# From the fourth block of tiles on, a pair of hidden cells is computed by seven half products

## The chip, the cores and the metric

The kernel runs on one core of a Trainium2 chip. Five engines work side by side and wait for each other by semaphores: PE (TensorE, matrix products into PSUM), ACT (ScalarE), DVE (VectorE), POOL (GpSimd) and SP (SyncE, which issues most transfers). The metric is the device time of one execution in microseconds (us); smaller is better.

## What is computed

A banded attention over 8 batches x 8 heads x 576 positions (head size 64, window 64), then a feed-forward layer on the 4608 tokens that it leaves:

```python
scores = np.where(mask, q @ k.transpose(0, 1, 3, 2) / 8.0, -1e9)   # mask: 0 <= i - j < 64
x = (softmax(scores) @ v).transpose(0, 2, 1, 3).reshape(4608, 512)
h = x @ w_in                                         # 512 x 2048
g = np.maximum(h, 0.0) + alpha * np.minimum(h, 0.0)
out = g @ w_out                                      # 2048 x 512
```

The weights are given in float64 and come to the chip as pairs of 32-bit words.

## The kernel before

**Tiles and blocks.** The 4608 tokens are 36 tiles of 128; four tiles are a block (`NBLK`), so there are nine blocks, numbered here from 0. The hidden size of 2048 is 16 slices f of 128 (`NF`). A *cell* is one block and one f (in block 0, for f below `PAIRS` = 4, two cells of two tiles each).

**A product in three parts.** x, w_in, w_out and g are each kept as a high part rounded to the matmul's format and a low part, the rest (`xh`/`xl`, `win_h`/`win_l`, `wout_h`/`wout_l`, `gh`/`gl`). A product is high x high + low x high + high x low. `weights` makes the parts of w_in and w_out from the 64-bit words in the first 130 us or so, and they stay in SBUF.

**A cell** (`cell`, L718) is this chain. PE: `hidden` (L726), 3 parts x 4 chunks of the contraction = 12 matmuls of a 128x128 weight with a moving operand of 512 tokens, into one PSUM bank `h`. ACT: `slopes` (L735) writes alpha times h to SBUF. DVE: `most` (L742) takes the larger of that and h. ACT: `high` (L748) rounds it to `gh`. POOL: `rest` (L752) makes `gl`. PE: `outs` (L757), 4 tiles x 3 parts = 12 matmuls of 512 columns that add to the four tiles' `o` banks over all f. After f = 15 ACT or DVE copies each `o` to SBUF and SP stores it. Four PSUM banks (4 to 7) are for `h`, scores and attention values, four for `o`.

**Attention of a tile** (`attend`, L474): PE scores (L571, many small matmuls), eight masks with row minimum on DVE (L605), eight exponentials on ACT (L611), a scale on POOL (L632), 12 transposes on DVE (L672), PE values `av` (L690), then `xh` on ACT (L694) and `xl` on DVE (L697). The tiles of block n are taken two at a time in blocks n - 2 and n - 1, at the places in `stays`.

**Order.** All steps are handed to a planner (`Plan`, L119) with an engine, a duration written in the code, predecessors and buffers. It lays them out in time, and the instructions are emitted in the order of the planned starts, so each engine's order is fixed before the run. For the steps of the first block, the weights and the first eight tiles, deadlines come from the table `DUE`. Waits on the chip are semaphores that the framework derives from which tiles an instruction reads and writes.

Of the kernel before, what the change touches and what calls it, by code (L numbers as in the profile page):

```python
# [278 lines left out]
def banded_attention_then_prelu_ffn(  # L279
# [438 lines left out]
    def cell(ts, f, want_h, want_o):  # L718
        plan.group = "c", f, ts[0]
        n = len(ts)  # L720
        nt = n * P
        d = {}
        xs = slice((ts[0] % RING) * P, (ts[0] % RING) * P + nt)
        hb, gb, ghb, glb = Buffer("bank", 1), Buffer("g", 1), Buffer("gh", 1), Buffer("gl", 1)

        def hidden(_):  # L726
            d["h"] = ph = bank(hb, [P, NBLK * P], F32, f"h_{ts[0]}_{f}")
            k = 0
            for wt, xt in (("win_h", xh), ("win_h", xl), ("win_l", xh)):
                for c in range(NP):  # L730
                    nc.tensor.matmul(ph[:, :nt], weight(wt, f)[:, c * P:(c + 1) * P], xt[:, c, xs],  # L731
                                     start=(k == 0), stop=(k == 3 * NP - 1))
                    k += 1
# [210 lines left out]
```

## Time and profile before

| | |
|---|---|
| median of 3 runs | 891.82 us (891.49 to 892.58) |
| the profiled execution, its own time | 889.84 us |
| its span, first to last instruction | 888.1 us |
| busy share of the span | PE 99%, DVE 48%, ACT 43%, POOL 36% |
| transfers | 69.8 MB, mean 79 GB/s |

The busy share of PE counts overlapping matmuls as they are modelled; what a matmul costs in a row of them is the distance from one start to the next, which the chain of work shows as a sum over its pieces. The chain is followed back from the last instruction, so a piece in it is time that the end of the kernel waits for. The rows themselves stand in the section after the change.

### The profile page before, as it was taken

To read this page: it belongs to the slowest core of one execution; us is meant where nothing else is said; L and a number is where in the kernel's file an instruction comes from. 1 tells how busy PE (TensorE), PEld (TensorE's weight loads), DVE (VectorE), ACT (ScalarE), POOL (GpSimd) and SP (SyncE) were. 2 spreads that over 40 slices of the span, in tenths; PEclk is the share of its full clock that TensorE was granted. 3 is DMA by queue.
4 is the path that set the end of the run, shared out by engine and by line. 5 is a ranking of instruction groups with operands and counts; after the bars stand their busy time and mean duration, and the time that the engine had idled before them with its cause. 6 is when DMAs were issued, how large, how long until landed. Compare 5 with 4: busy or idle time off the path is not lost.

```text
span 888.1 us, 17218 instructions
## 1 busy us (share of the span) xinstructions
PE 881.9 (99%) x6785; PEld 731.7 (82%) x6785; DVE 423.3 (48%) x1326; ACT 378.5 (43%) x1023; POOL 322.1 (36%) x293
## 2 busy tenths in 40 slices
PE   9999999999999999999999999999999999999998
PEld 8888888888888888888888888888888888888886
DVE  6989864767262634444362617172535345111111
ACT  7888855424342434242433324253424252222222
POOL 5878743333333333323241333233333222222221
PEclk9999999999999999999999999999999999999999
DMA  9656743313130304030220213031303030001001
GB/s 325 213 189 199 240 136 102 70 40 90 66 90 18 91 30 126 18 91 18 79 77 26 66 66 90 18 90 66 90 18 90 18 97 1 1 1 48 1 1 48
DMA packets 55393, 69.80 MB, mean 79 GB/s; under 512 B 3456, under 2 KB 48784, under 8 KB 55312
## 3 DMA queue, kind: packets, MB, share of 16 engines
q1 hardware_dynamic: 54576, 68.04, 25.2%
q8 instruction: 53, 0.87, 0.4%
q10 hardware_dynamic: 736, 0.66, 0.2%
q14 instruction: 28, 0.23, 0.1%
HBM read 59.25 MB, written 9.44 MB: 77 GB/s over the span
## 4 chain that ended last, share of the span: by engine, by line
PE 98%; DVE 1%; ACT 0%; issue 0%; POOL 0%; ACTq 0%; DVEq 0%; POOLq 0%
PE h L731 44%; PE o L769 44%; PE av L690 4%; PE s L571 3%; PE s L553 1%; PE spare L363 1%; PE t L649 1%; DVE w L595 0%; ACT w L601 0%; DVE two L398 0%; ACT pt L654 0%; POOL w L632 0%; DVE rc L627 0%; DVE xl L697 0%; DVE val L415 0%
## 5 line engine op out<-in xcount | busy, mean ns | idle before, releaser
L754 POOL TENSOR_TENSOR gl<-g,gh 128x512 fp32r<-128x512 f32 x128 | 165.1, 1290 | 367.9 <-ACT gh L750 228.4
L744 DVE SCALAR_TENSOR_TENSOR g<-h,s_sb,g 128x512 f32<-128x512 f32 x128 | 96.0, 751 | 305.8 <-ACT g L737 305.7
L769 PE MATMUL o<-wout_h,gh 128*128 128x512 f32 x576 | 225.3, 391 | 0.0
L769 PE MATMUL o<-wout_l,gh 128*128 128x512 f32 x576 | 224.3, 389 | 0.0
L737 ACT ACTIVATE g<-h,sa_sb 128x512 f32<-128x512 f32 (+1 forms) x148 | 100.2, 677 | 245.3 <-PE h L731 223.8
L769 PE MATMUL o<-wout_h,gl 128*128 128x512 f32 x576 | 159.1, 389 | 0.0
L731 PE MATMUL h<-xh,win_h 128*128 128x512 f32 (+1 forms) x592 | 157.3, 388 | 0.0
L731 PE MATMUL h<-xl,win_h 128*128 128x512 f32 (+1 forms) x592 | 155.0, 384 | 0.0
L731 PE MATMUL h<-xh,win_l 128*128 128x512 f32 (+1 forms) x592 | 154.8, 383 | 0.0
L750 ACT CAST gh<-g 128x512 fp32r<-128x512 f32 x128 | 79.4, 620 | 130.4 <-DVE g L744 78.4
L672 DVE STREAM_TRANSPOSE pt<-w 32x256 f32<-32x256 f32 x312 | 130.1, 428 | 4.6 <-POOL w L632 0.9
L731 PEld LDWEIGHTS h<-xl,win_h 128*128 128x128 f32 x592 | 109.5, 188 | 22.2
L731 PEld LDWEIGHTS h<-xh,win_l 128*128 128x128 f32 x592 | 109.5, 188 | 21.9
L731 PEld LDWEIGHTS h<-xh,win_h 128*128 128x128 f32 x592 | 108.2, 188 | 23.2 <-DVE gl L754 0.2
L769 PEld LDWEIGHTS o<-wout_h,gh 128*128 128x128 f32 x576 | 108.1, 188 | 22.7 <-issue 0.5
L769 PEld LDWEIGHTS o<-wout_h,gl 128*128 128x128 f32 x576 | 108.1, 188 | 22.6
L769 PEld LDWEIGHTS o<-wout_l,gh 128*128 128x128 f32 x576 | 108.2, 188 | 22.1
L611 ACT ACTIVATE w<-w,nm 128x96 f32<-128x96 f32 x208 | 75.5, 365 | 93.1 <-DVE nm L605 93.1
L632 POOL TENSOR_TENSOR w<-w,rc 128x768 f32<-128x768 f32 (+2 forms) x44 | 59.3, 1348 | 137.9 <-ACT w L611 105.9
L605 DVE CUSTOM_DVE_ANT_0 w<-s,masks 128x96 f32<-128x96 f32 x184 | 34.4, 253 | 91.1 <-PE s L571 91.1
L419 POOL TENSOR_TENSOR val<-val,low 128x512 int32<-128x512 int32 x32 | 41.2, 1293 | 13.2 <-DVE val L415 7.6
L690 PE MATMUL av<-pt,v 128*64 128x64 f32 x1152 | 38.8, 224 | 0.5 <-ACT pt L654 0.5
(65 smaller groups left out, 593.5 us busy)
## 6 DMA issues: line engine op xcount, KB each, us to landing
v<-vN SPq DMA_DIRECT2D x72, 256.0 KB, 4.5
k<-kT SPq DMA_DIRECT2D x35, 384.0 KB, 5.1
out<-os SPq DMA_DIRECT2D x35, 256.0 KB, 2.1
q<-qT SPq DMA_DIRECT2D x34, 256.0 KB, 6.2
raw<-w_in SPq DMA_DIRECT2D x16, 512.0 KB, 4.6
raw<-w_out SPq DMA_DIRECT2D x16, 512.0 KB, 3.9
k<-kT SPq DMA_DIRECT2D x2, 192.0 KB, 3.2
q<-qT ACTq DMA_DIRECT2D x2, 128.0 KB, 3.4
```

What stands on the lines that cost most here:

```text
L419: nc.gpsimd.tensor_tensor(out=d["val"], in0=d["val"], in1=d["tail"], op=ALU.add)
L605: nc.vector.tensor_tensor_reduce(out=d["w"][:, e, h], in0=d["s", e][:, h], in1=slim[begins], op0=ALU.add, op1=ALU.min, scale=-SCALE, scala ...
L611: nc.scalar.activation(w, w, AF.Exp, scale=-1.0, bias=d["nm"][:, g:g + 1], accum_out=d["sm"][:, g:g + 1])
L632: nc.gpsimd.tensor_tensor(out=w, in0=w, in1=d["rc"][:, g].unsqueeze(2).broadcast_to(list(w.shape)), op=ALU.mult)
L672: nc.vector.transpose(dst[:, :, i * SUB:(i + 1) * SUB], d["w"][r, :, :, k * SUB:(k + 1) * SUB].rearrange("p e h k -> p (e h) k"))
L690: nc.tensor.matmul(av[r, e, u * W:(u + 1) * W], d["v"][:, e, u, r], d["pt"][:, u * NP + e, h * W:(h + 1) * W], start=True, stop=True)
L731: nc.tensor.matmul(ph[:, :nt], weight(wt, f)[:, c * P:(c + 1) * P], xt[:, c, xs], start=(k == 0), stop=(k == 3 * NP - 1))
L737: nc.scalar.activation(d["g"], d["h"][:, :nt], AF.Copy, scale=sa_sb[:, f:f + 1])
L744: nc.vector.scalar_tensor_tensor(out=g, in0=d["h"][:, :nt], scalar=s_sb[:, f:f + 1], in1=d["g"], op0=ALU.mult, op1=ALU.max)
L750: nc.scalar.copy(d["gh"], d["g"])
L754: (nc.vector if start else nc.gpsimd).tensor_tensor(out=d["gl"], in0=d["g"], in1=d["gh"].bitcast(F32), op=ALU.subtract)
L769: nc.tensor.matmul(po[t], gt[:, i * P:(i + 1) * P], weight(wt, f), start=(f == 0 and k == 0), stop=(f == NF - 1 and k == 2))
```

## The change

From block 3 on (`W0`), two neighbouring cells f and f + 1 are one `pair`. h is then a 2 x 2 of blocks (two slices f, two halves of 256 tokens), and the contraction has two halves of 256; the eight half products of such a 2 x 2 are replaced by seven, in Winograd's form of Strassen's algorithm, whose operands are sums of blocks of w_in and sums of blocks of x. A half product (`product`) is 3 parts x 2 chunks = 6 matmuls of a 128x128 weight with 256 tokens.

*Sums of w_in.* `combine`, once for each of the eight pairs of slices, after block 0: the four sums are formed on POOL and DVE, split into parts on ACT and POOL or DVE, and SP writes them to a DRAM tile `kept`, five entries of 256 KB in all for a pair of slices. In each of the six blocks each pair reads its five entries back (`load`, 240 reads) into five buffers. The part of the resident w_in that is no longer read becomes room for these and for the sums of x.

*Sums of x.* In `attend`, for every second tile from tile 13 on, DVE forms sums of x (`t_one`, `t_two`), and ACT and DVE split them (`t_high`, `t_low`); the even tile's PSUM bank is kept until then.

*A pair* has two banks: bank X holds a (right half) and b (left half), bank Y holds c (right half) and d (left half). The products are emitted on PE in the order p12 (two: into a, and into b), p7 (into d), p6 (onto a), p4 (onto d), p5 (onto a), p3 (onto a). Between them ACT copies half a bank to SBUF (`spare`, 128x256), and DVE adds it (`add`, 128x256): c1 copies a after p12 and v1 adds it to b; c7 copies d after p7; c6 copies a after p6; v2 makes c from a after p5; v3 adds to d after p4. `behind` is the old chain of a cell after `hidden`; in a pair its `outs` is cut in three steps.

```diff
+W0 = 3
+SHORT = 93.0
+TSETS = (0, 3)
+LAGS = (16.0, 19.0)
...
+    dram = ctx.enter_context(tc.tile_pool(name="dram", bufs=1, space=bass.MemoryType.DRAM))
...
-        ab, xb = Buffer("bank", 1), Buffer(f"x{t % RING}", 1)
+        paired = t >= W0 * NBLK
+        slot = t // NBLK % 2 * NBLK + ((0, 2, 1, 3)[t % NBLK] if paired else t % NBLK)
+        ab, xb = Buffer("bank", 1), Buffer(f"x{slot}", 1)
         d["x"] = xb
-        xs = slice((t % RING) * P, (t % RING + 1) * P)
+        xs = slice(slot * P, (slot + 1) * P)
...
-        hi = step({ACT: (0.47, 0.59)}, x_high, [va], take=[xb])
-        return scores, va, step({DVE: (0.6, 0.69)}, x_low, [hi], give=[ab], want=want)
+        d["va"], d["ab"] = va, ab
+        if not paired:
+            hi = step({ACT: (0.47, 0.59)}, x_high, [va], take=[xb])
+            return scores, va, step({DVE: (0.6, 0.69)}, x_low, [hi], give=[ab], want=want)
+        if t % 2 == 0:
+            hi = step({ACT: (0.47, 0.59)}, x_high, [va], take=[xb])
+            d["low"] = step({DVE: (0.6, 0.69)}, x_low, [hi], want=want)
+            return scores, va, d["low"]
...
+        def whole(_):
+            d["x32"] = room(xt, [P, E], F32, f"x32_{t}")
+            nc.scalar.copy(d["x32"], d["av"].rearrange("p k w -> p (k w)"))
+        def t_one(_):
+            a, b, (x1, _x2) = d0["av"], d["av"], halves()
+            sub(a[:, 0:2], x1, a[:, 0:2])
+            sub(b[:, 0:2], b[:, 2:4], x1)
+
+        def t_two(_):
+            a, (_x1, x2) = d0["av"], halves()
+            sub(x2, x2, a[:, 0:2])
+            sub(a[:, 2:4], a[:, 2:4], x2)
+        def t_high(m):
+            nc.scalar.copy(turns("win_h", q0 + (m == 1) * 2, m), pieces(m))
+        def t_low(m):
+            q = q0 + (m == 1) * 2
+            sub(turns("win_l", q, m), pieces(m), turns("win_h", q, m).bitcast(F32))
+        w0 = step({ACT: (0.48, 0.59)}, whole, [va], take=[xt])
+        one = step({DVE: (0.78, 0.88)}, t_one, [d0["va"], w0, d0["low"]])
+        hi = step({ACT: (0.47, 0.59)}, x_high, [one], take=[xb])
+        two = step({DVE: (0.78, 0.88)}, t_two, [one])
+        lo = step({DVE: (0.6, 0.69)}, x_low, [hi], give=[ab])
+        ha = step({ACT: (0.47, 0.59)}, lambda _: t_high(2), [two], take=[tsets[n]] if j == 0 else [])
+        hb = step({ACT: (0.28, 0.39)}, lambda _: t_high(1), [two], [ha])
+        la = step({DVE: (0.6, 0.69)}, lambda _: t_low(2), [ha, lo], give=[d0["ab"]], want=want)
+        lb = step({DVE: (0.33, 0.42)}, lambda _: t_low(1), [hb, la], give=[xt], want=want)
+        return scores, va, lb
...
+    def behind(ts, f, d, done, hb, want_o, cols, coarse=True):
...
+        every = [(i, k) for i in range(n) for k in (0, 1, 2)]
+        gh_ones, gl_ones = [x for x in every if x[1] < 2], [x for x in every if x[1] == 2]
+        if f == NF - 1:
+            todos = [every] if coarse else [every[j:j + 3] for j in range(0, 3 * n, 3)]
+        else:
+            todos = [gh_ones + gl_ones] if coarse else [gh_ones[:4], gh_ones[4:], gl_ones]
...
+        for todo in todos:
+            lows = any(k == 2 for _, k in todo)
+            h = 0.68 * n if coarse else 0.2267 * len(todo)
+            own = sorted({ts[i] for i, k in todo if f == 0 and k == 0})
+            s5 = step({PE: (h, h + 0.1)}, lambda _, todo=todo: outs(todo),
+                      [s3] + [s4] * lows + cv[2 * f + 1]["done"], take=[ob[t] for t in own],
+                      give=[ghb] + [glb] * lows, want=want_o)
...
+    def combine(q):
+        plan.group = "s", q, 2 * NBLK
+        d = {}
...
+        def total(e, i):
+            d[i] = room(bufs[i], [P, E], F32, f"sum_{q}_{i}")
+            (nc.gpsimd if e == POOL else nc.vector).tensor_tensor(
+                out=d[i], in0=weight("win_h", f + i).bitcast(F32), in1=weight("win_l", f + i).bitcast(F32), op=ALU.add)
+
+        def sums(_):
+            a11, a12, a21, a22 = d[0][:, :2 * P], d[0][:, 2 * P:], d[1][:, :2 * P], d[1][:, 2 * P:]
+            nc.vector.tensor_tensor(out=a22, in0=a21, in1=a22, op=ALU.add)
+            nc.vector.tensor_tensor(out=a21, in0=a11, in1=a21, op=ALU.subtract)
+            nc.vector.tensor_tensor(out=a11, in0=a22, in1=a11, op=ALU.subtract)
...
+        entries[q] = dram.tile([P, 5, 2, 2 * P], F32, name=f"kept_{q}")
+        t0 = step({POOL: (1.22, 1.28), DVE: (0.59, 0.68)}, lambda e: total(e, 0), done, begun[-NBLK:],
+                  take=bufs + taken.get(q, []), give=regions[q], port=True)
+        begun.append(t0)
+        t1 = step({POOL: (1.22, 1.28), DVE: (0.59, 0.68)}, lambda e: total(e, 1), [*done, t0], give=regions[q], port=True)
+        su = step({DVE: (1.35, 1.45)}, sums, [t0, t1], port=True)
+        out = [step({SP: (0.4, 0.4)}, lambda _, low=low: keep(2, low), done, [t0], give=regions[q], moved=0.6, span=0.8)
+               for low in (0, 1)]
+        for i in range(2):
+            hi = step({ACT: (0.51, 0.61)}, lambda _, i=i: high(i), [su])
+            lo = step({POOL: (1.22, 1.28), DVE: (0.59, 0.68)}, lambda e, i=i: rest(e, i), [hi], port=True)
+            out.append(step({SP: (0.4, 0.4)}, lambda _, i=i: keep(i, 0), [hi], give=[bufs[2 + i]], moved=0.9))
+            out.append(step({SP: (0.4, 0.4)}, lambda _, i=i: keep(i, 1), [lo], give=[bufs[i]], moved=0.9))
+        kept[q] = out
+
...
+    def pair(ts, q, want):
+        plan.group = "c", 2 * q, ts[0]
+        n = ts[0] // NBLK
+        f = 2 * q
+        dx, dy, d = {}, {}, {}
+        bx, by, u2 = Buffer("bank", 1), Buffer("bank", 1), Buffer("u2", 1)
+        left = slice(ts[0] % RING * P, ts[0] % RING * P + 2 * P)
+        right = slice(left.stop, left.stop + 2 * P)
+        q0 = TSETS[(n - W0) % 2]
+
+        def load(e):
+            def fetch(_):
+                where = b.at
+                d[e] = (region("win_" + where[0], where[1]) if isinstance(where, tuple) else
+                        room(b, [P, E], F32R, f"stream_{n}_{q}_{e}"))
+                nc.sync.dma_start(d[e].bitcast(F32).rearrange("p (l c) -> p l c", l=2), entries[q][:, e])
+
+            s = step({SP: (0.4, 0.4)}, fetch, kept[q], loaded[-1:], take=[b], moved=0.85, span=1.1)
+            loaded.append(s)
+            return s, b
...
+        def product(out, w, x, start):
+            todo = [(w[i], x[j]) for i, j in ((0, 0), (0, 1), (1, 0))]
+            for i, (a, b) in enumerate(todo):
+                for c in range(2):
+                    nc.tensor.matmul(out, a[:, c * P:(c + 1) * P], b[c], start=start and i == c == 0,
+                                     stop=i == 2 and c == 1, skip_group_check=True)
+
+        def p12(_):
+            dx["h"] = bank(bx, [P, NBLK * P], F32, f"h_{ts[0]}_{f}")
+            d["b"], d["a"] = dx["h"][:, :2 * P], dx["h"][:, 2 * P:]
+            product(d["a"], own(0, 0), tokens(0, left), True)
+            product(d["b"], streamed(0), tokens(1, left), False)
+
+        def p7(_):
+            dy["h"] = bank(by, [P, NBLK * P], F32, f"h_{ts[0]}_{f + 1}")
+            d["d"], d["c"] = dy["h"][:, :2 * P], dy["h"][:, 2 * P:]
+            product(d["d"], streamed(3), tokens(0, right), True)
+
+        def p6(_):
+            product(d["a"], streamed(1), turned(2), False)
+
+        def p5(_):
+            product(d["a"], streamed(4), turned(0), False)
+
+        def p3(_):
+            product(d["a"], streamed(2), tokens(1, right), False)
+
+        def p4(_):
+            product(d["d"], own(1, 1), turned(1), False)
+
+        def add(out, a, b):
+            nc.vector.tensor_tensor(out=out, in0=a, in1=b, op=ALU.add)
+
+        def spare(i, x):
+            if "u" not in d:
+                d["u"] = room(u2, [P, E], F32, f"u_{n}_{q}")
+                d["u"] = d["u"][:, :2 * P], d["u"][:, 2 * P:]
+            nc.scalar.copy(d["u"][i], d[x])
...
+        one = {PE: (0.72, 0.87)}
+        s12 = step({PE: (1.44, 1.59)}, p12, [st_done[t] for t in ts] + [l0], take=[bx], give=[b0, x0, x2], want=want)
+        s7 = step(one, p7, [l3], [s12], take=[by], give=[b3, x1, x3], want=want + 1.0)
+        c1 = step({ACT: (0.28, 0.39)}, lambda _: spare(1, "a"), [s12], take=[u2])
+        c7 = step({ACT: (0.28, 0.39)}, lambda _: spare(0, "d"), [s7], [c1])
+        v1 = step({DVE: (0.38, 0.48)}, lambda _: add(d["b"], d["b"], d["u"][1]), [c1])
+        s6 = step(one, p6, [c1, l1], [s7], give=[b1, tsets[n]], want=want + 2.0)
+        c6 = step({ACT: (0.28, 0.39)}, lambda _: spare(1, "a"), [s6, v1])
+        s5 = step(one, p5, [c6, l4], give=[b4, tsets[n]], want=want + 3.0)
+        s4 = step(one, p4, [c7], give=[tsets[n]], want=want + 4.0)
+        v2 = step({DVE: (0.38, 0.48)}, lambda _: add(d["c"], d["a"], d["u"][0]), [s5, c7])
+        s3 = step(one, p3, [v2, l2], [s4], give=[b2, x1, x3], want=want + 5.0)
+        v3 = step({DVE: (0.38, 0.48)}, lambda _: add(d["d"], d["d"], d["u"][1]), [s4, c6, v2], give=[u2])
+        first[n, f] = first[n, f + 1] = s12
...
+        cols = (0, 2, 1, 3)
+        behind(ts, f, dx, [s3, v1], bx, want + LAGS[0], cols, False)
+        behind(ts, f + 1, dy, [v2, v3], by, want + LAGS[1], cols, False)
...
+            if n >= W0:
+                if f % 2 == 0:
+                    pair(ts, f // 2, at(n, f) - 5.0 * (n == NB - 1 and f == NF - 2))
```

**PE, one pair.** The first place is on PE in the last block, around slices 4 and 5. In the names, `h_32_4` is the bank of block 8 (its first tile is 32), f = 4, which is X; `h_32_5` is Y; `wout`, `gh`, `gl` are as above; `stream` and `win_l_12`, `win_h_14`, ... are buffers that hold read-back sums; where `win_h` stands on the left of a comma it is the moving operand, a sum of x. A bracket lists the semaphores that the first matmul of a row waits for. Before, a cell and what follows it:

```order
L731 MATMUL h_32_4_8236<-xh_96,win_h_92 128x512 x4
L731 MATMUL h_32_4_8236<-xl_97,win_h_92 128x512 x4
L731 MATMUL h_32_4_8236<-xh_96,win_l_93 128x512 x4
L769 MATMUL o_32_8149<-wout_h_94,gh_32_3_8232 128x512 [waits Activation_49]
L769 MATMUL o_32_8149<-wout_l_95,gh_32_3_8232 128x512
```

After, from the end of p12 over p7, p6 and p4 to the first of p5:

```order
L1009 MATMUL h_32_4_9820<-xh_98,stream_8_2_0_9739 128x256 x2
L1009 MATMUL h_32_5_9835<-xh_98,win_h_12_1332 128x256 [waits DMAHW5_49,PE_49]
L1009 MATMUL h_32_5_9835<-xh_98,win_h_12_1332 128x256
L1009 MATMUL h_32_5_9835<-xl_99,win_h_12_1332 128x256 x2
L1009 MATMUL h_32_5_9835<-xh_98,win_h_12_1332 128x256 x2
L1009 MATMUL h_32_4_9820<-win_h_94,win_l_12_1334 128x256 [waits DMAHW7_49,DVE_49]
L1009 MATMUL h_32_4_9820<-win_h_94,win_l_12_1334 128x256
L1009 MATMUL h_32_4_9820<-win_l_95,win_l_12_1334 128x256 x2
L1009 MATMUL h_32_4_9820<-win_h_94,win_l_12_1334 128x256 x2
L1009 MATMUL h_32_5_9835<-win_h_94 128x256 [waits Activation_49]
L1009 MATMUL h_32_5_9835<-win_l_95,win_h_94 128x256 x2
L1009 MATMUL h_32_4_9820<-win_h_94,win_h_14_1640 128x256 [waits DMAHW0_49,Activation_49]
```

Where a cell's 12 matmuls ran without a wait, p6 now waits for a count of DVE; in the program it is reached by v1, the add to b, though p6 writes a: both lie in bank X. Of the 48 pairs, 38 have this wait on v1. In the other 10 p6 waits for c1 on ACT, and v1 waits for the end of p6; p5 then waits for c6, which comes after v1. Between the end of p12 and p6 stands p7 alone in 39 pairs (29 of the 38, and the 10); in 9 pairs `outs` of an earlier cell stands there too.

**DVE, the same pair.** The second place is DVE at the same slices. Before, one instruction for a cell:

```order
L744 SCALAR_TENSOR_TENSOR g_32_2_8197<-h_32_2_8172,s_sb_83,g_32_2_8197 128x512 [waits Activation_49]
L744 SCALAR_TENSOR_TENSOR g_32_3_8229<-h_32_3_8204,s_sb_83,g_32_3_8229 128x512 [waits Activation_49]
L744 SCALAR_TENSOR_TENSOR g_32_4_8261<-h_32_4_8236,s_sb_83,g_32_4_8261 128x512 [waits Activation_49]
L744 SCALAR_TENSOR_TENSOR g_32_5_8293<-h_32_5_8268,s_sb_83,g_32_5_8293 128x512 [waits Activation_49]
L744 SCALAR_TENSOR_TENSOR g_32_6_8325<-h_32_6_8300,s_sb_83,g_32_6_8325 128x512 [waits Activation_49]
```

After, the three adds v1, v2, v3 (`u` is the SBUF copy) and the two cells' `most`:

```order
L1036 TENSOR_TENSOR h_32_4_9820<-h_32_4_9820,u_8_2_9842 128x256 [waits Activation_49]
L1036 TENSOR_TENSOR h_32_5_9835<-h_32_4_9820,u_8_2_9842 128x256 [waits DVE_49,PE_49,Activation_49]
L1036 TENSOR_TENSOR h_32_5_9835<-h_32_5_9835,u_8_2_9842 128x256 [waits DVE_49,Activation_49]
L804 SCALAR_TENSOR_TENSOR g_32_5_9880<-h_32_5_9835,s_sb_85,g_32_5_9880 128x512 [waits Activation_49]
L804 SCALAR_TENSOR_TENSOR g_32_4_9899<-h_32_4_9820,s_sb_85,g_32_4_9899 128x512 [waits Activation_49]
```

v1 waits for c1 on ACT, and c1 for the end of p12: PE, ACT, DVE and PE again follow each other.

**ACT, where attention runs.** The third place is ACT around the attention of tiles 20 to 23, in block 4. Before:

```order
L694 CAST xh_96<-av_20_4805 128x4x128 [waits PE_49]
L611 ACTIVATE w_22_4770,sm0_87<-w_22_4770,nm0_86 128x96 [waits DVE_49]
L694 CAST xh_96<-av_21_4829 128x4x128 [waits PE_49]
L611 ACTIVATE w_22_4770,sm0_87<-w_22_4770,nm0_86 128x96 [waits DVE_49] x5
L611 ACTIVATE w_23_4855,sm1_90<-w_23_4855,nm1_89 128x96 [waits DVE_49] x3
L737 ACTIVATE g_16_4_4939<-h_16_4_4894,sa_sb_85 128x512 [waits PE_49,Pool_49]
```

After:

```order
L702 CAST xh_98<-av_21_5332 128x4x128 [waits DVE_49]
L617 ACTIVATE w_23_5356,sm1_92<-w_23_5356,nm1_91 128x96 x2
L757 CAST win_h_94<-av_20_5306 128x2x2x128 [waits DVE_49]
L1042 COPY u_4_2_5459<-h_16_4_5430 128x256 [waits PE_49,Activation_49]
L757 CAST win_h_94<-x32_21_5391 128x2x128 [waits Activation_49]
L1042 COPY u_4_2_5459<-h_16_5_5449 128x256 [waits PE_49]
L617 ACTIVATE w_23_5356,sm1_92<-w_23_5356,nm1_91 128x96
L1042 COPY u_4_2_5459<-h_16_4_5430 128x256 [waits DVE_49]
```

The copies that PE now waits for (L1042) stand in one queue with the exponentials and with the splitting of the sums of x.

## Rows read from the trace of the kernel before

**Rows 1.** The page: engines' busy time, and the chain that ended last, by engine.

```profile
PE 881.9 (99%) x6785; PEld 731.7 (82%) x6785; DVE 423.3 (48%) x1326; ACT 378.5 (43%) x1023; POOL 322.1 (36%) x293
PE 98%; DVE 1%; ACT 0%; issue 0%; POOL 0%; ACTq 0%; DVEq 0%; POOLq 0%
```

**Rows 2.** Waits of PE's own: engine line, waited for: total us, times, longest.

```profile
PE t L649 <- POOL w L632: 0.7, 1, 0.7
PE av L690 <- ACT pt L654: 0.5, 1, 0.5
```

**Rows 3.** The chain in order of time: start us, us, what.

```profile
36.73 1.43 PE h L731 x12
250.90 2.94 PE h L731 x12
391.02 8.38 PE h L731 x36
486.25 8.39 PE h L731 x36
789.34 2.72 PE h L731 x12
792.06 2.72 PE o L769 x12
```

**Rows 4.** Groups, shapes apart: line engine op xcount | busy, mean ns | idle before.

```profile
L804 ACT COPY os<-o 128x256 f32<-128x256 f32 x1 | 0.4, 372 | 0.7 <-DVE os L806 0.7
L754 DVE TENSOR_TENSOR gl<-h,gh 128x256 fp32r<-128x256 f32 x8 | 3.3, 417 | 0.4 <-ACT gh L750 0.4
L744 DVE SCALAR_TENSOR_TENSOR h<-h,s_sb,g 128x256 f32<-128x256 f32 x8 | 3.9, 485 | 0.7 <-ACT g L737 0.6
```

**Rows 5.** Timeline of the last block: start us, us, engine line op [idle before <-releaser].

```profile
813.66 0.39 PE L769 MATMUL o<-wout_h,gh 128*128 128x512 f32 x1
813.92 0.69 ACT L737 ACTIVATE g<-h,sa_sb 128x512 f32<-128x512 f32 x1 [3.31 <-PE h L731]
814.64 0.75 DVE L744 SCALAR_TENSOR_TENSOR g<-h,s_sb,g 128x512 f32<-128x512 f32 x1 [4.69 <-ACT g L737]
815.42 0.62 ACT L750 CAST gh<-g 128x512 fp32r<-128x512 f32 x1 [0.82 <-DVE g L744]
```

**Rows 6.** Timeline: two idle times of PE, with releasers, and a transpose without.

```profile
27.33 1.04 POOL L632 TENSOR_TENSOR w<-w,rc 128x512 f32<-128x512 f32 x1 [0.87 <-DVE rc L628]
28.43 0.66 PE L649 MATMUL t<-ident,w 128*128 128x128 f32 x4 [0.69 <-POOL w L632]
29.17 0.58 ACT L654 COPY pt<-t 128x512 f32<-128x512 f32 x1
29.81 1.04 PE L690 MATMUL av<-pt,v 128*64 128x64 f32 x28 [0.46 <-ACT pt L654]
...
122.79 0.60 PE L649 MATMUL t<-ident,w 128*128 128x128 f32 x4
```

**Rows 7.** Timeline: weight loads and matmuls of a 256-token cell.

```profile
36.92 0.55 PEld L731 LDWEIGHTS h<-xl,win_h 128*128 128x128 f32 x4
37.04 0.64 PE L731 MATMUL h<-xl,win_h 128*128 128x256 f32 x4
```

**Rows 8.** Groups, shapes apart: attention's work on ACT and DVE.

```profile
L672 DVE STREAM_TRANSPOSE pt<-w 32x256 f32<-32x256 f32 x312 | 130.1, 428 | 4.6 <-POOL w L632 0.9
L611 ACT ACTIVATE w<-w,nm 128x96 f32<-128x96 f32 x208 | 75.5, 365 | 93.1 <-DVE nm L605 93.1
L697 DVE TENSOR_TENSOR xl<-av,xh 128x512 fp32r<-128x512 f32 x36 | 24.9, 690 | 17.0 <-ACT xh L694 17.0
L694 ACT CAST xh<-av 128x512 fp32r<-128x512 f32 x36 | 21.0, 584 | 10.2 <-PE av L690 10.1
```

**Rows 9.** Busy us by stretch: PE, PEld, DVE, ACT, POOL, clock, DMA.

```profile
112.00:205.00 93.00, 92.90 (x871) 76.34 (x870) 57.54 (x206) 46.44 (x146) 35.41 (x32) 1.00 0.34 94
300.00:395.30 95.30, 95.30 (x770) 79.01 (x769) 42.82 (x143) 35.76 (x104) 30.13 (x28) 1.00 0.22 63
```

**Rows 10.** Transfers: engine op xcount, KB each, median us from issue to landing.

```profile
v<-vN SPq DMA_DIRECT2D x72, 256.0 KB, 4.5
```

More of the change, by code (lines that the diff above doesn't have):

```diff
@@ L716, in parts @@
         return [slice(0, E // 2), slice(E // 2, E)] if t == NT - 1 else [slice(0, E)]
-    def cell(ts, f, want_h, want_o):
-        plan.group = "c", f, ts[0]
+    def behind(ts, f, d, done, hb, want_o, cols, coarse=True):
         n = len(ts)
         nt = n * P
[L722 to L733, printed above, removed]
+        gb, ghb, glb = Buffer("g", 1), Buffer("gh", 1), Buffer("gl", 1)
         def slopes(_):
@@ L777, in cell @@
                 ob[t] = Buffer("o", len(parts(t)))
-        s0 = step({PE: (hold[0], lat[0])}, hidden, [st_done[t] for t in ts] + cv[2 * f]["done"], take=[hb],
-                  want=want_h)
-        first[ts[0] // NBLK, f] = s0
-        for b in xb:
-            b.uses = NF
-        s0.give += xb
-        s1 = step({ACT: (hold[1], lat[1])}, slopes, [s0], take=[gb])
+        s1 = step({ACT: (hold[1], lat[1])}, slopes, done, take=[gb])
         s2 = step({DVE: (hold[2], lat[2])}, most, [s1], give=[gb] if start else [hb])
@@ L788, in cell @@
                   give=[hb if start else gb])
-        s5 = step({PE: (0.68 * n, 0.68 * n + 0.1)}, outs, [s3, s4] + cv[2 * f + 1]["done"],
-                  take=[ob[t] for t in ts] if f == 0 else [], give=[ghb, glb], want=want_o)
-        for x in {id(last_o[t]): last_o[t] for t in ts if t in last_o}.values():
-            s5.behind.append(x)
-            x.before.append(s5)
-        for t in ts:
-            last_o[t] = s5
+        ghb.uses = len(todos)
+        glb.uses = sum(any(k == 2 for _, k in todo) for todo in todos)
+        whole = {}
+        for todo in todos:
[5 more added lines that the diff above has]
+                      give=[ghb] + [glb] * lows, want=want_o)
+            for x in {id(last_o[t]): last_o[t] for t in ts if t in last_o}.values():
+                put_behind(s5, x)
+            for t in ts:
+                last_o[t] = s5
+            whole.update({ts[i]: s5 for i, k in todo if k == 2})
         if f == NF - 1:
@@ new lines, in cell, with hidden @@
+    def cell(ts, f, want_h, want_o):
+        plan.group = "c", f, ts[0]
+        n = len(ts)
+        nt = n * P
+        d = {}
+        xs = slice((ts[0] % RING) * P, (ts[0] % RING) * P + nt)
+        hb = Buffer("bank", 1)
+        def hidden(_):
+            d["h"] = ph = bank(hb, [P, NBLK * P], F32, f"h_{ts[0]}_{f}")
+            k = 0
+            for wt, xt in (("win_h", xh), ("win_h", xl), ("win_l", xh)):
+                for c in range(NP):
+                    nc.tensor.matmul(ph[:, :nt], weight(wt, f)[:, c * P:(c + 1) * P], xt[:, c, xs],
+                                     start=(k == 0), stop=(k == 3 * NP - 1))
+                    k += 1
+        xb = [st[t]["x"] for t in ts]
+        s0 = step({PE: ({2: 1.46, 4: 2.72}[n], {2: 1.55, 4: 2.87}[n])}, hidden,
+                  [st_done[t] for t in ts] + cv[2 * f]["done"], take=[hb], want=want_h)
+        first[ts[0] // NBLK, f] = s0
+        for b in xb:
+            b.uses = NF
+        s0.give += xb
+        if ts[0] // NBLK == W0 - 1:
+            s0.give += regions[f // 2]
+        behind(ts, f, d, [s0], hb, want_o, range(n))
@@ L819, in load_alpha @@
+    tsets, loaded, last_p = {}, [], {}
+    regions, taken, begun = {}, {}, []
+    for i, q0 in enumerate(TSETS):
+        b = Buffer(f"reg{i}", 3 * 6, f"T{i}")
+        taken[q0] = [b]
+        regions.update({q: [b] for q in range(q0, q0 + 3)})
+    for q in (6, 7):
+        taken[q] = regions[q] = [Buffer(f"ring{2 * q - 6 + i}", 6, "ring") for i in range(2)]
     def load_alpha(_):
```

98 lines of the change are left out of this document (81 added, 17 removed).

## The prediction

> **What bounds the kernel now.** I read the page first. PE is busy for 99% of the span, DVE, ACT and POOL for half of it or less, and PE holds 98% of the chain that ended last, so the end moves only with PE's stream: its work, or a wait put into it [rows 1]. Then PE's own waits: the four behind the attention's small products sum to 2.5 us in the whole run, the two largest being 0.7 and 0.5 us [rows 2]. So there is almost no idle time to give back; the change has to win by removing PE work and loses whatever it makes PE wait.
>
> The chain in order of time gives the prices. In the last block the two products of a cell take 2.72 us each [rows 3], that is 2.72 / 12 = 0.227 us for a matmul of 512 tokens. A 256-token cell of block 0 takes 1.43 us, 0.119 us a matmul [rows 3]. A `hidden` right after attention takes 2.94 us, 0.22 more [rows 3]. The same place of two following blocks (36 matmuls) starts at 391.02 and at 486.25: a block is 95.2 us [rows 3], of which 16 x 5.44 = 87.0 are cells and 8.2 is attention. The granted clock is 1.00 (2.4 GHz) in both stretches of [rows 9], and I leave it there.
>
> **1. The work removed.** A pair before is two `hidden`, 2 x 2.72 = 5.44 us. After it is seven half products, 42 matmuls of 256 tokens: 42 x 0.119 = 5.00 us. `outs` stays the same 12 matmuls a cell. So a pair saves 0.435 us on PE, not an eighth of 5.44 (0.68), because a half-wide matmul costs more than half a wide one. Six blocks of eight pairs are 48 pairs: **-20.9 us**.
>
> What would halve exactly is a matter of a fixed cost for each matmul. The Trainium skill, "TensorE: Matmul & The Clock Gate", section "Back-to-back issue gap", gives the isolated gap as N / 2.4 GHz + about 2.5 ns, which is an estimate of 109.2 ns for 256 and 215.8 ns for 512 columns; the gain would be 48 x (24 x 0.2158 - 42 x 0.1092) = 28.5 us, 7.6 more than mine. The trace disagrees with it, 119 and 227 ns, and the trace decides.
>
> **2. The wait before p6.** Before, a `hidden` never waited for DVE. Now p12 ends, c1 (ACT) copies a, v1 (DVE) adds it to b, and in 38 of 48 pairs p6 waits for v1, since a and b share bank X. I count from the end of p12, which is the start of p7 on PE:
> - to the start of c1: PE starts `outs` at 813.66 and ACT starts on the h before it at 813.92, 0.26 us [rows 5];
> - c1, a copy of 128x256 out of PSUM on ACT: 0.372 us [rows 4];
> - ACT to DVE: ACT ends at 814.61 and DVE starts at 814.64, 0.03 us [rows 5];
> - v1, 128x256 on DVE with one operand in PSUM: 0.417 us by the tensor_tensor, 0.485 by the scalar_tensor_tensor [rows 4];
> - release of PE: 0.06 us, the same from POOL (28.37 to 28.43) and from ACT (29.75 to 29.81) [rows 6].
>
> That is 1.14 to 1.21 us. What covers it is p7 alone in 39 of the pairs: 6 x 0.119 = 0.715 us. PE stands still for 0.42 to 0.49 us. Then it has to start again: four transposes after such a wait take 0.66 us, without it 0.60 [rows 6], and a weight load that normally starts 0.12 us ahead of its matmul [rows 7] may be late by that. So the stall is between 0.42 and 0.61 us; I take 0.52, the middle of 0.42 to 0.49 with the 0.06 of the transposes. In 29 of these 39 pairs it stands at p6. In the 10 others p6 waits for c1 only, but v1 then waits for the end of p6 and c6 for v1, so p5 waits for the same four steps, with p4 (0.715 us) as its cover: the same stall, one product later. In the remaining 9 pairs an `outs` of 2.72 us stands in the gap as well, and the wait is nothing. Sum: 39 x 0.52 = **+20.3 us** (16.4 to 23.8). What waits behind p6 on PE is everything, since PE's order is fixed.
>
> That p6 waits for an add into another half of its bank is needed by a rule in the Trainium skill, "PSUM — Partial Sum Buffer", section "Terms": two engines on one bank at once are an error. No run here shows it. By it alone, halves in different banks would leave the wait on c1 (next paragraph), about 20 us less than my sum.
>
> **3. Waits that are almost covered.** Where only a copy lies between two products (a PE end, c1 or c6, a PE start), the path is 0.26 + 0.372 + 0.06 = 0.69 us against a cover of 0.715. That fits by 0.02, but the weight load wants to start 0.12 ahead [rows 7], so each such place costs 0 to 0.10. There are 44 (p5 on c6 with p4 as cover, or p6 on c1): 0 to 4.4, I take **+2**. p3's wait for v2 (c6, p5, v2) has `outs` pieces in front, 0.91 us or 2.72, and costs nothing; if these pieces were gone it would cost as p6 does.
>
> **4. Attention's stretches.** The copies and adds stand in the queues of ACT and DVE behind exponentials of 0.365 us and transposes of 0.428 us [rows 8]. In addition ACT gets for every odd tile a copy, a split like `xh` (0.584) and a half one (0.372), DVE two times two subtractions and one and a half splits like `xl` (0.690) [rows 4, 8]. By share that fits: DVE was busy 42.8 and ACT 35.8 of 95.3 us in a block [rows 9]; per block DVE gains 24 adds x 0.417 = 10.0 and 2 x 2.8 of sums, ACT 24 copies x 0.372 = 8.9 and 2 x 1.5, so 58 and 48 of some 95. But one operation in front of c1 or v1 lengthens a stall by itself: about two pairs a block by 0.4 and one by 0.1, in the five blocks (3 to 7) in which attention still runs: 4.5, I take **+4** (1 with a queue mostly empty, 8 with four pairs a block).
>
> **5. Switches of PE between cells and attention's small products.** The order on PE has 78 of them in place of 60, nine more stays at 0.22 us each (the 2.94 against 2.72): **+2** (1 to 4, if each of the 18 switches cost 0.22).
>
> **6. The sums of w_in.** In blocks 1 and 2 `combine` adds for each of eight pairs of slices four 128x512 operations on POOL (1.04 us each, as the scale of [rows 6]; 33 us in all), three 128x256 ones on DVE (10 us) and two copies on ACT (9 us). Between 112 and 205 us POOL was busy 35.4, DVE 57.5, ACT 46.4 of 93 us [rows 9], and there are two such blocks: it fits beside PE, whose cells there have no new wait. **+0.5** (0 to 2). If it didn't fit, `gl` on POOL would be late and each cell would wait.
>
> **7. Read-back.** Each pair reads 5 x 256 KB. At about 11.3 us a pair that adds 113 GB/s to the 63 of [rows 9], with two thirds of the transfer engines' time free there (share 0.22). A 256 KB transfer lands in a median 4.5 us [rows 10], and a buffer is free some 10 us before its next content is needed. I take 0; with the lead gone, every pair would wait for up to 4.5 us. These reads stand in SP's queue, whose other work there is the loads of v and the stores, none of which PE waited for [rows 2].
>
> **Sum.** -20.9 + 20.3 + 2 + 4 + 2 + 0.5 = **+7.9 us**. The profiled execution took 889.84 us, 2.0 less than the median of the runs, so its successor would be 897.7 and the median **about 900 us**. With all terms at their low ends the median is 889.3, at their high ends 913.1.
>
> **Rivals.**
> - *B, the other side: the wait on v1 doesn't end last.* If the path from p12 to p6 were 0.715 us or less (c1 and v1 quicker, or the handoff from PE counted twice), the whole of term 2 falls: 900 - 20.3 = **879** (873 to 889). It decides below a stall of (20.9 - 8.5) / 39 = 0.32 us, where the change breaks even. For it: each handoff was read from one place, and the four steps would have to shrink by 0.1 to 0.2 us only to reach that point. Against: c1 and v1 alone, without any handoff, are 0.79 us, already more than the cover.
> - *C: ACT's and DVE's queues become the bound.* If c1 or v1 finds one operation of 0.37 in front of it in all 48 pairs and not in a few, term 4 becomes 17.5: **913**. For it: the order on ACT puts exponentials and copies in turn. Against: both engines stay near half busy, and the last block has no attention.
> - *D: a half-wide matmul costs half.* At 0.113 us a pair saves 0.68, in all 32.6, 11.8 more: **888**. For it: the 0.119 is from the first 40 us, where other work shares SBUF. Against: PE never idled inside those 12. The rule cited under 1 would lie near this one, at 892.
> - That the change does less than it says would show as fewer than 48 pairs; the order has all 48.
>
> **Chances.** The forecast 0.62, B 0.18, C 0.12, D 0.08. The range is 879 to 914: it leaves out half of B, most of the upper part of C and the very ends of the forecast's own. What a measurement of this kernel tells from no change is about 0.2%, 890.0 to 893.6. Faster than that: B, D and the lowest tip of the forecast, 0.28; within: 0.08; slower: 0.64.
>
> **What would show it.** In the changed trace the 256-token matmuls (L1009) should take 0.715 us for six; ACT's copies (L1042) about 0.37, DVE's adds (L1036) about 0.42; among PE's waits one group at L1009 should name DVE's L1036, with some 29 waits near 0.5 us, and one ACT's L1042, with 10 such and many of near 0. Blocks 3 to 8 should each be 1 to 2 us longer than 95.2. If PE's waits at L1009 sum to less than 10 us, term 2 is wrong; if they exceed 30, C is right; if the six take 0.68, D. Waits on read-back transfers above a few us would show term 7 wrong, and any growth of blocks 1 and 2 term 6.

## The result, and the profile after

| | before | changed | ratio (95% interval) |
|---|---|---|---|
| median | 891.9 us | 904.9 us (902.4 to 906.2) | 1.0142 (1.0119 to 1.0164) |
| span of the profiled execution | 888.1 us | 904.5 us | |

The change makes the kernel 13.0 us slower; the forecast was 7.9. The profiled execution is the slowest of the changed kernel's four (906.2 us), so the spans differ by 16.4 us.

The changed kernel's page answers to [rows 1]: engines' busy time, and the chain that ended last, by engine.

```profile
PE 879.7 (97%) x7649; PEld 761.5 (84%) x7649; DVE 541.8 (60%) x1581; ACT 454.7 (50%) x1227; POOL 346.0 (38%) x310
PE 87%; DVE 4%; ACT 3%; DMA 3%; issue 1%; POOL 0%; ACTq 0%; DVEq 0%; POOLq 0%
```

DVE and ACT are still busy for only 60 and 50% of the time, but they now hold 7% of the chain. That is the mark of a handoff, not of a full engine. PE's own waits (engine line, waited for: total us, times, longest) say where; before, all four summed to 2.5 us (those of [rows 2], and 1.1 us and 0.2 us at the start of the kernel):

```profile
PE h L1009 <- DVE h L1036: 8.0, 30, 0.6
PE h L895 <- DVE nm L611: 3.0, 2, 1.6
PE h L1009 <- ACT u L1042: 2.7, 10, 0.3
PE s L559 <- DMA q<-qT: 1.2, 1, 1.2
```

Thirty waits on the adds and ten on the copies: all but one of them are the pairs of the prediction's second term. The timeline places 29 at p6 and ten at p5, the 39 that were worked out; the thirtieth is a p3 that waits for v2. The chain of work, in order of time (start us, us, what), walks through one of them in the last block:

```profile
872.58 1.45 PE h L1009 x12
874.02 0.02 issue
874.04 0.02 ACTq L1042
874.06 0.04 issue
874.10 0.38 ACT u L1042
874.48 0.02 issue
874.51 0.44 DVE h L1036
874.95 0.04 issue
874.99 2.42 PE h L1009 x18
877.41 2.74 PE o L831 x12
```

p12, c1, v1, p6 follow each other. p7 is not in the chain, since it ends before v1 does; the timeline has its first matmul here:

```profile
873.85 0.40 PE L1009 MATMUL h<-xh,win_h 128*128 128x256 f32 x2
```

What that costs on PE is read from the timeline of another block (start us, us, engine line op, idle before and its releaser):

```profile
569.45 0.40 PE L1009 MATMUL h<-xh,win_h 128*128 128x256 f32 x2
569.69 0.40 PE L1009 MATMUL h<-xl,win_h 128*128 128x256 f32 x2
569.70 0.37 ACT L1042 COPY u<-h 128x256 f32<-128x256 f32 x1 [1.81 <-PE h L1009]
569.93 0.40 PE L1009 MATMUL h<-xh,win_h 128*128 128x256 f32 x2
570.11 0.43 DVE L1036 TENSOR_TENSOR h<-h,u 128x256 f32<-128x256 f32 x1 [2.87 <-ACT u L1042]
570.36 0.37 ACT L1042 COPY u<-h 128x256 f32<-128x256 f32 x1 [0.29 <-PE h L1009]
570.59 0.51 PE L1009 MATMUL h<-win_h,win_l 128*128 128x256 f32 x2 [0.27 <-DVE h L1036]
570.94 0.40 PE L1009 MATMUL h<-win_l,win_l 128*128 128x256 f32 x2
571.17 0.40 PE L1009 MATMUL h<-win_h,win_l 128*128 128x256 f32 x2
```

Two half-wide matmuls start 0.24 us after the two before them; this is the undisturbed pace (569.45, 569.69, 569.93). The next two come after 0.66: a stall of 0.42. The two behind them come after 0.35: the first matmul of p6 loses 0.11 more. So a wait that the table of waits puts at 0.27 costs 0.53. The table counts from the modelled end of the last matmul, and a matmul's end lies about 0.16 us behind the point at which the next could have started. For a busy PE, stalls are better read from start to start.

Doing that for every matmul of both traces (the distance from each start to the next; of it, 0.2267 us for a 512-column and 0.1192 us for a 256-column one is called work and the rest a gap) gives the difference of the spans:

| part of PE's time | before | changed | difference |
|---|---|---|---|
| work of `outs` | 391.5 | 391.5 | 0.0 |
| work of h (wide, and seven half products) | 392.3 | 371.4 | -20.9 |
| gaps at half products | | 23.4 | +23.4 |
| gaps at `outs` | 4.4 | 8.8 | +4.4 |
| gaps at the h of whole cells | 3.1 | 4.9 | +1.8 |
| scores, with the pauses behind them | 35.2 | 40.1 | +4.9 |
| other small products | 56.6 | 57.9 | +1.3 |
| before the first matmul, and from the last one's start | 5.1 | 6.4 | +1.3 |
| sum | 888.1 | 904.5 | +16.4 |

Not all of this is the pairs'. In block 0 the 192nd matmul of `outs` starts at 133.5 us, before at 129.8, and no pair has run by then; in the traces of the runs below it starts between 130.9 and 134.7. So some of these 3.7 us belong to this one execution.

By blocks, counted by 192 matmuls of `outs`: the stretch of block 2 goes from 95.2 to 101.4 us, those of blocks 4 to 6 only to 96.1, 95.9 and 95.9. (The stretches of blocks 1 and 3, 106.0 to 100.5 and 95.2 to 100.7, can't be read so: the place of `outs` in the order moved there.) So in blocks 4 to 6 the pairs by themselves cost 0.7 to 0.9 us a block, and block 2, which has hardly a pair, loses some 6. The windows there (busy us of PE, PEld, DVE, ACT, POOL, then PE's granted clock, DMA share, GB/s) and the timeline show what happened:

```profile
268.00:269.00 1.00, 0.52 (x20) 0.31 (x20) 0.00 (x0) 1.00 (x5) 0.00 (x0) 1.00 0.84 265
269.00:270.00 1.00, 0.00 (x0) 0.00 (x0) 0.98 (x8) 0.58 (x4) 0.00 (x0) 1.00 1.15 251
270.00:271.00 1.00, 0.37 (x2) 0.36 (x3) 0.97 (x5) 0.65 (x2) 0.00 (x0) 0.99 1.06 185
271.00:272.00 1.00, 1.00 (x4) 0.81 (x3) 1.00 (x5) 0.99 (x4) 0.00 (x0) 0.50 1.02 268
273.00:274.00 1.00, 1.00 (x4) 0.78 (x3) 0.80 (x7) 0.64 (x4) 0.02 (x1) 0.50 1.03 286
274.00:275.00 1.00, 1.00 (x5) 0.81 (x4) 0.00 (x0) 0.00 (x0) 1.00 (x1) 0.81 1.07 390
```

```profile
269.56 0.42 DVE L726 TENSOR_TENSOR av<-x,av 128x256 f32<-128x256 f32 x1
269.89 0.43 DVE L726 TENSOR_TENSOR av<-av,x 128x256 f32<-128x256 f32 x1
270.23 0.25 DVE L611 CUSTOM_DVE_ANT_0 w<-s,masks 128x96 f32<-128x96 f32 x1
270.63 1.74 PE L895 MATMUL h<-xh,win_h 128*128 128x512 f32 x4 [1.64 <-DVE nm L611]
```

After two tiles' scores PE has nothing for 1.64 us, because a cell's h waits for DVE to read the scores. Of the four banks for h, scores and values, the next scores hold two and the values of tiles 12 and 13 hold the others. In the planner's layout of the kernel before, the first h behind the scores takes tile 12's bank, which is free once `xl` is made. Now that bank is kept until the sums of x are formed, so this h has to take a bank of the scores, which is free after four masks (L611); and two subtractions of the sums (L726) stand in DVE's queue in front of the fourth. Then the granted clock falls from 1.00 to 0.50 (2.4 to 1.2 GHz) between 271.0 and 274.4 us, in which PE has work; this costs about 1.6 us, the gaps at the wide h from 130 us on being 2.1 us here and 0.5 in the traces of runs 3 and 4, where the clock stayed at 1.00. A second such wait, 1.35 us, stands in front of 304.92.

### The profile page after: what moved, and what is told of

It is laid out like the page before. It is cut to its first block, busy times and chain, and to the rows that moved or that the text cites. A ratio compares the mean times of both kernels' runs of the same rounds, so it can differ in the third digit from the quotient of the medians.

```text
span 904.5 us, 20317 instructions
## 1 busy us (share of the span) xinstructions
PE 879.7 (97%) x7649; PEld 761.5 (84%) x7649; DVE 541.8 (60%) x1581; ACT 454.7 (50%) x1227; POOL 346.0 (38%) x310
## 4 chain that ended last, share of the span: by engine, by line
PE 87%; DVE 4%; ACT 3%; DMA 3%; issue 1%; POOL 0%; ACTq 0%; DVEq 0%; POOLq 0%
PE o L831 42%; PE h L1009 25%; PE h L895 13%; PE av L698 3%; PE s L577 3%; DVE h L1036 2%; ACT u L1042 2%; DMA raw<-w_in 1%; DMA raw<-w_out 1%; PE s L559 1%; DMA q<-qT 1%; PE t L655 1%; PE spare L369 0%; DVE two L404 0%; DVE two L412 0%
## 5 line engine op out<-in xcount | busy, mean ns | idle before, releaser
L1036 DVE TENSOR_TENSOR h<-h,u 128x256 f32<-128x256 f32 x144 | 62.0, 430 | 181.5 <-PE h L1009 109.4
L678 DVE STREAM_TRANSPOSE pt<-w 32x256 f32<-32x256 f32 x312 | 127.4, 424 | 5.4 <-POOL w L638 1.1
L1042 ACT COPY u<-h 128x256 f32<-128x256 f32 x144 | 53.8, 374 | 127.6 <-PE h L1009 120.8
L1009 PE MATMUL h<-win_h,win_l 128*128 128x256 f32 x288 | 61.4, 295 | 7.4 <-DVE h L1036 7.4
L1009 PE MATMUL h<-xh,win_l 128*128 128x256 f32 x288 | 57.8, 282 | 0.6 <-DVE h L1036 0.6
L1009 PE MATMUL h<-xh,win_h 128*128 128x256 f32 x288 | 57.7, 282 | 0.0
L895 PE MATMUL h<-xh,win_h 128*128 128x512 f32 (+1 forms) x208 | 54.0, 382 | 3.0 <-DVE nm L611 3.0
L1009 PEld LDWEIGHTS h<-win_h,win_l 128*128 128x128 f32 x288 | 44.2, 190 | 13.3 <-DVE h L1036 13.3
L895 PE MATMUL h<-xl,win_h 128*128 128x512 f32 (+1 forms) x208 | 53.1, 378 | 0.0
L895 PE MATMUL h<-xh,win_l 128*128 128x512 f32 (+1 forms) x208 | 52.5, 374 | 0.0
```

The costliest lines, as they stand in the source:

```text
L678: nc.vector.transpose(dst[:, :, i * SUB:(i + 1) * SUB], d["w"][r, :, :, k * SUB:(k + 1) * SUB].rearrange("p e h k -> p (e h) k"))
L1009: nc.tensor.matmul(out, a[:, c * P:(c + 1) * P], b[c], start=start and i == c == 0, stop=i == 2 and c == 1, skip_group_check=True)
L1036: nc.vector.tensor_tensor(out=out, in0=a, in1=b, op=ALU.add)
L1042: nc.scalar.copy(d["u"][i], d[x])
```

## The experiments

All times are medians, with the ratio to the kernel before and its interval. The kernel before was run again beside them and took 891.7 and 892.0 us, so the changed kernel's 904.9 can be set beside these times as well.

**1. The planner is told of v1.** p6 waits on the chip for v1, since both write bank X, but the planner had only c1 as its predecessor. This run corrects that and nothing else.

```diff
-        s6 = step(one, p6, [c1, l1], [s7], give=[b1, tsets[n]], want=want + 2.0)
+        s6 = step(one, p6, [c1, l1, v1], [s7], give=[b1, tsets[n]], want=want + 2.0)
```

> The changed kernel with one word more for the planner: p6 (s6) has v1 among its predecessors. Nothing is computed differently; the planner now puts a piece of outs between p12 and p6, so that the least cover of the wait for v1 grows from 0.72 to 1.62 us of PE work in all 48 pairs. Theory (the stall at p6 and p5 is what the seven products cost): the 40 stalls, 21 us in the changed kernel's trace counting the slow first matmul behind each, shrink to the almost covered waits, under 4 us in sum; about 905 - 18 = 887 us, faster than the kernel before. Rival (the stall only stands where another limit, ACT's and DVE's queues or the read-back, would hold PE a little later): the waits move to other releasers and the time stays at 900 to 905.

Measured: **885.1 us**, 0.9928 (0.9909 to 0.9948), 19.8 us less than the changed kernel, and faster than before. Its waits of PE:

```profile
PE h L895 <- DVE nm L611: 3.0, 2, 1.6
PE h L1009 <- ACT u L1042: 1.4, 1, 1.4
PE spare L369 <- DVE xl L368: 1.1, 1, 1.1
```

Of the thirty waits on L1036 one of 0.2 us is left, of the ten on a copy one, and the two for banks in block 2 stand as they did. The gaps at half products, counted as above, fall from 23.4 to 3.5 us. Copies, adds, products and read-back are all the same and only their order moved, so it is the place of p6 behind too little cover, and not the load of ACT and DVE, that cost 20 us.

**2. v1 left out.**

```diff
-        v1 = step({DVE: (0.38, 0.48)}, lambda _: add(d["b"], d["b"], d["u"][1]), [c1])
+        v1 = step({DVE: (0.38, 0.48)}, lambda _: None, [c1])
```

> The changed kernel without v1: b lacks the added a, so this part of the result is missing; every other instruction stands where it stood. p6 then waits for c1 alone, against a cover of 0.715 us. Theory (v1 is what makes c1's path too long): the 30 stalls of about 0.55 us at p6 and, since c6 no longer follows v1, the 10 at p5 fall to 0 to 0.1 each; 905 - 18 = 887 us, within 2 us of the run in which v1 is covered. If instead p6 still stands for 0.3 us or more behind c1, the handoff from PE to ACT is longer than the 0.26 us that I took, and the time stays above 893.

Measured: **888.4 us**, 0.9968 (0.9954 to 0.9982). Nothing moved but v1, and 16.5 us are gone. So v1 is what makes the path too long. It stays 3.3 us above run 1, where at most 2 were expected: with p6 on c1 and p5 on c6 the path of some 0.69 us meets the cover of 0.715, and the trace has 72 gaps of about 0.065 us between half products, 4.7 us in all, where run 1 has none of that size. A cover that equals the path isn't free. One wait of PE on L1036 stays, 0.6 us: it is that of p3 on v2.

**3. v1 done twice.**

```diff
-        ... lambda _: add(d["b"], d["b"], d["u"][1]), [c1])
+        ... lambda _: [add(d["b"], d["b"], d["u"][1]) for _ in range(2)], [c1])
```

> The changed kernel with v1 done twice (b gets a added twice, so the result is off by that); the planner's order is as it was. It doubles the suspected cost: one more 128x256 add of about 0.42 us on the path from p12 to p6 (and in ten pairs from p6 to p5). Theory: the 39 or 40 stalls grow by 0.42 to 0.43 each, 17 us, so about 922 us, with the 30 waits of PE for L1036 near 0.7 in the place of 0.27 us each. Rival (the stall has another floor, the first read-back or c7, behind which v1 hides in part): less than 10 us more.

Measured: **926.1 us**, 1.0380 (1.0365 to 1.0396), 21.2 us more than the changed kernel, where 17 were expected. Its waits of PE, and the two adds on DVE:

```profile
PE h L1009 <- ACT u L1042: 31.0, 39, 1.1
564.93 0.90 DVE L1036 TENSOR_TENSOR h<-h,u 128x256 f32<-128x256 f32 x2 [1.74 <-PE h L1009]
```

The mean wait rises from 10.7 / 40 = 0.27 to 31.0 / 39 = 0.79. In this program the wait on DVE is an instruction of its own in front of p6, and the matmul itself waits for c1; the table names only the latter, which had long been done. Two adds take 0.90 us where one takes 0.43. Read from start to start, with the slow first matmul behind them, the 39 stalls at p6 and p5 rise from 20.4 to 40.5 us, 0.51 each; all gaps at half products rise by 21.8, since the almost covered places also rise, from 11 to 43. p3's wait for v2 stays as it was. The direction and the size agree: 0.47 us more on this path costs some 20 us.

**4. The banks of tiles 12 and 14 given back early.** For the even tiles of block 3, ACT copies the values to SBUF once `xl` is made, and the sums use the copy.

```diff
-            d["low"] = step({DVE: (0.6, 0.69)}, x_low, [hi], want=want)
+            aside = t // NBLK == W0
+            d["low"] = step({DVE: (0.6, 0.69)}, x_low, [hi], give=[ab] * aside, want=want)
+            if aside:
+                d["ab"] = xe = Buffer("os", 1)
+                def away(_):
+                    y = room(xe, [P, NP, P], F32, f"x32_{t}")
+                    nc.scalar.copy(y, d["av"])
+                    d["av"] = y
+                ab.uses = 2
+                d["va"] = d["low"] = step({ACT: (0.48, 0.59)}, away, [d["low"]], take=[xe], give=[ab], want=want)
```

> The changed kernel in which, for the two even tiles of block 3 (12 and 14), ACT copies av to SBUF and gives the bank back, and the sums of x are taken from that copy. Theory (in block 2 a cell's h waits for a bank because scores hold two of four and the even tile's av, kept for the sums, a third and the odd tile's a fourth; PE stood 1.6 and 1.4 us there and the granted clock then fell to 0.50 for some 3.5 us): both waits and the low clock go, 4 to 6 us less, about 899 to 901 us. Rival (DVE's queue, not the bank, is late): the waits stay, 904 to 906 us.

Measured: **901.0 us**, 1.0108 (1.0089 to 1.0126), 3.9 us less than the changed kernel: within what was expected, at its smaller end. Its waits of PE (L1020, L1047, L1053 and L906 are L1009, L1036, L1042 and L895 of the changed kernel) and the stretch of the first stall, first in this run and then in the changed kernel:

```profile
PE h L1020 <- DVE h L1047: 8.3, 30, 0.6
PE h L1020 <- ACT u L1053: 3.5, 10, 1.0
PE h L906 <- DVE nm L611: 1.0, 1, 1.0
262.00:280.00 18.00, 16.80 (x237) 13.96 (x218) 15.71 (x59) 12.61 (x44) 7.30 (x7) 1.00 0.60 175
```

```profile
262.00:280.00 18.00, 15.87 (x237) 12.79 (x236) 11.73 (x52) 11.42 (x43) 3.82 (x3) 0.91 0.64 184
```

The low clock is gone, of the two waits in block 2 (1.64 and 1.35 us) 1.0 and 0.2 are left, and the forty stalls of the pairs stand as they did, but for a longest of 1.0. The edit moves two things, though, since the sums now wait for ACT's copy:

```profile
267.09 1.17 PE L906 MATMUL h<-xh,win_h 128*128 128x512 f32 x4 [0.98 <-DVE nm L611]
267.57 0.42 DVE L737 TENSOR_TENSOR x<-x,x 128x256 f32<-128x256 f32 x1
298.69 1.19 PE L906 MATMUL h<-xh,win_h 128*128 128x512 f32 x4 [0.25 <-ACT x L724]
```

At the first place h still waits for the masks, and so for a bank of the scores; the wait is shorter because the sums (L737) now stand behind the masks. At the second it waits only for the copy that frees tile 14's bank (L724): there it is the bank. How the 3.9 us divide between the bank and the place of the sums on DVE, this run doesn't show.

**5. No pairs at all.** `W0 = 9`: `combine` runs, and all cells are whole.

> The changed kernel with W0 = 9: all blocks are computed by whole cells as before, while combine still forms w_in's sums in blocks 1 and 2 and writes them to DRAM; nothing reads them. It separates what the preparation and the changed order of the first blocks cost from what the pairs cost. Theory (combine is hidden beside PE, and the 6 us lost in block 2 come from the attention of the first paired tiles): 892 to 894 us, no change against before beyond 2 us. Rival (combine delays g or gl, or its traffic delays loads): 896 to 900 us.

Measured: **893.4 us**, 1.0022 (1.0011 to 1.0033): 1.8 us above before, 1.0 to 2.9 by the interval. From the start of the last matmul of `outs` to the end it takes 5.3 us, as in the changed kernel, against 4.0 before: an `o` of 512 columns is now copied last, behind the two halves of the last tile. So 1.3 us of it are the order of the last copies, and little (0.4 us, which the interval doesn't tell from nothing) is left for `combine`; its traffic and its 33 us on POOL lie beside PE's work.

**6. Pairs from block 6 on.** `W0 = 6`.

> The changed kernel with W0 = 6: three blocks of pairs (6 to 8) and not six. With W0 = 9 it took 893.4, with W0 = 3 904.9: 11.5 us for six blocks. Theory (a fixed part of about 4 us for the banks in the block before the first pairs, and 7.5 us / 6 = 1.25 us for each block of pairs): 893.4 + 4 + 3.8 = about 901 us. Rival (no fixed part, 1.9 us a block): 899 us; rival (only the blocks 3 to 5, beside the combine's end and the first read-back, lose): 894 to 896 us.

Measured: **901.1 us**, 1.0095 (1.0074 to 1.0116), on the expected 901. Three blocks of pairs cost 7.7 us above run 5 and three more only 3.7: a fixed part of some 4 us and some 1.2 us a block. The waits have the same two kinds, fewer of the one and as large a one of the other:

```profile
PE h L1009 <- DVE h L1036: 4.9, 18, 0.6
PE h L895 <- DVE xl L705: 2.4, 2, 1.8
PE h L895 <- DVE nm L611: 1.4, 1, 1.4
```

**7. Both remedies** (the edits of 1 and 4).

> Both remedies in one kernel: the planner knows v1 (885.06 us alone) and the banks of tiles 12 and 14 are given back early (3.9 us less alone). Theory (the two costs stand in different blocks and add up): 885.1 - 3.9 = about 881 us, 1.2% faster than before. Rival (with the stalls gone the lost time in block 2 is caught up behind another limit): 884 to 886 us.

Measured: **882.1 us**, 0.9890 (0.9871 to 0.9909), 9.9 us faster than before and 22.8 us faster than the changed kernel. Alone the two remedies gave 19.8 and 3.9, together 23.7, so they add up within the spread of the runs: the two costs are independent.

## Why the prediction was right, and where it was short

The sign, the mechanism and the range were right. The forecast of +7.9 us was 5.1 short of the measured 13.0, not because of the stalls but because of costs that it did not have.

1. *The work removed, -20.9.* The changed trace has 2016 half-wide matmuls (48 x 42), and undisturbed ones start 0.119 to 0.120 us apart: the step holds, and with it the answer to rival D. The 119 ns of block 0 [rows 3] is the price in the middle of the kernel too, and the formula of the Trainium skill, "TensorE: Matmul & The Clock Gate", section "Back-to-back issue gap", by which the gain would have been 28.5 us, does not fit this stream.
2. *The wait before p6, +20.3.* PE stands 29 times at p6 and 10 times at p5, as read from the order. In the row of 874 us the path is 0.38 + 0.03 + 0.44 + 0.04 from c1 on, and p7 starts at 873.85, so 0.25 to c1: 1.14 us, the low end of the 1.14 to 1.21 worked out. The stalls are 0.36 to 0.45 (mean 0.42) and the slow restart 0.10, so 0.52, as forecast; 39 of them are 20.4 us. That it fits to a hundredth is in part luck: the stall was taken too large, the middle of 0.42 to 0.49, and the restart too small, 0.06 [rows 6], when it is near the 0.12 of a late weight load [rows 7]. Rival B falls with this, and runs 1 to 3 show the cause by removing and by doubling it. What was put at nothing is p3's wait for v2: in one place no piece of `outs` stands in front, and it cost 0.84 us.
3. *Almost covered waits, +2.* The price of 0 to 0.10 was right (0.065 where they occur), their number not: 11 in the changed kernel, 0.7 us. Where v1 is absent there are 72.
4. *Attention's stretches, +4.* This step failed. The queues of ACT and DVE cost little: the gaps at half products are 3.6 us in each of blocks 4 to 6, 4.2 in block 7 and 3.8 in block 8, which has no attention; only block 3 has more, 4.8. What attention did cost is in block 2, and it was not a queue in front of c1 or v1 but the bank of h and the sums in front of the mask that frees it. The change keeps the even tile's bank; this stood in front of the prediction and was given no price. Run 4's edit takes back 3.9 us, the largest part of the missing 5.1.
5. *Switches, +2.* The first matmul on either side of attention is late by about 0.1 us, on 19 more sides: 1.9 us. What was not foreseen: `outs` behind half products take 2.73 to 2.75 us (877.41 above) and not the 2.72 of [rows 3]. A few hundredths in each of 96 make some 2.4 us; no run shows why.
6. *Sums of w_in, +0.5.* Run 5 allows 0.4 us or so beside the last copies, which the prediction did not look at: 1.3 us.
7. *Read-back, 0.* No wait on a `kept` transfer stands among PE's waits. They land in a median 2.7 to 2.9 us.

Rival C would have shown over 30 us of waits at L1009; 10.7 stand there. Two of the prediction's signs misled. Blocks 3 to 8 were to be 1 to 2 us longer each, and blocks 4 to 6 are 0.7 to 0.9. Growth of blocks 1 and 2 was to show term 6 wrong, but run 5 clears `combine`: block 2 grew by the waits for banks. Its reading of [rows 2] has a slip that changes nothing: the largest of the four waits is 1.1 us, of a filler matmul at the start.

That the sum came within 5 us of the result also owes something to luck. Terms 3 and 4 were some 4 us too high, and what was missing (the banks 3.9, `outs` 2.4, the last copies 1.3, p3 0.8) makes 8.4.

## What to carry to other kernels

A fast algorithm that saves 8% of one stage's work (0.435 of 5.44 us here) has less to give than one handoff through two other engines costs (1.15 us), so each handoff needs other work of that length behind it on the busy engine, in the fixed order. Who plans that order must know every wait that the chip will see, also those that come from two halves of one bank and not from the data; one missing predecessor was the difference between 1.4% slower and 0.7% faster. Count the banks that a new lifetime holds at the moment when the others are all taken.
